# An RWKV-6 attention with a two-layer network behind it: the same 1124 steps in another order, 39 of them on another engine

## The chip, the cores and the metric

The kernel runs on one core of a Trainium2 chip. The metric is the device time of one execution in microseconds (us). One execution was also profiled, and its trace gives the begin and length of each instruction on each engine. PE is TensorE (matrix products and transposes), DVE is VectorE, ACT is ScalarE, POOL is GpSimd, and SP is the engine that issues the transfers (DMA).

## What is computed

The first part is a recurrence with one state of 48 x 48 for each of 4 batches and 8 heads, over 768 positions. The second part takes the result as 3072 rows of 384 numbers through two matrices with a leaky ReLU between them.

```python
for t in range(S):                       # S = 768; B = 4, H = 8, D = 48
    cur = einsum('bhd,bhe->bhde', u * k_t, v_t)
    y[:, :, t] = einsum('bhd,bhde->bhe', r_t, state + cur)
    state = w_t[..., None] * state + einsum('bhd,bhe->bhde', k_t, v_t)
x = y.transpose(0, 2, 1, 3).reshape(3072, 384)
h = x @ w_in                             # 384 x 2048
out = maximum(0.01 * h, h) @ w_out       # 2048 x 384
```

## The kernel before

**Chunks.** The positions are cut into pieces of 128 rows, so that a piece of all eight heads is one tile of 128 x 384. Inside a piece the recurrence becomes matrix products. The logarithms of the decays w are taken (L508, L718) and summed down the rows by a product with a triangular matrix (L518, L724). ACT takes exponentials of the sums (L551 in `pair`, L750 and L754 in `single`). DVE multiplies r and k with them (the four multiplications at L407 of a `pair`, two of a `single` chunk). PE transposes the products (L418), they are copied out of PSUM to `g` or `rkT` by ACT (L425) or DVE (L423), and PE forms the scores (L632, L864). DVE masks the scores (L644, L795), PE multiplies them with v (L657, L836), and the bonus of u comes from POOL (L437, L441, L449) and a DVE sum (L445). The state `s` is carried from one chunk to the next: `sb` is the state times its decay (L602, L782), PE sums the new one into PSUM (L591, L609, L805), and a copy, a "keep", puts it back into SBUF (L617 on DVE or L619 on ACT in `pair`; L818 and L820 in `single`).

**Pairs and singles.** The function `pair` does the first chunks of two batches at once, with 64 rows each, at the head of the program. `single` does one chunk of 128 rows for later ones. Its transposed r and k come either through PE and a copy, or by a DMA transpose (L771) that SP issues. The result y (L482, L688) has to be transposed too, by PE (L468, copied by L473 on DVE or L475 on ACT) or by a DMA transpose (L849).

**The network.** For each block of rows, "up" is the product with w_in (L1030), ACT applies the leaky ReLU (L1045), and "down" is the product with w_out (L1060), whose result is copied to `o` and stored (L1077). The last seven blocks use another form for the second layer, `seven`, which makes seven products out of sums of matrix pieces: DVE makes the sums of pieces of 128 x 1024 (L941), PE multiplies (L960), the results are added by DVE (L981) after copies (L974, L976), and L1013 stores them. The weights are loaded as float32 (L318, L323) and cast to bfloat16 by POOL (L340), DVE (L342) or ACT (L344).

**What sets the order.** Each piece of work is a step in a list of 1124, with the engines that may do it. A table `ORDER` gives the order in which the steps are issued, and a table `FORCE` the engine of those that have a choice. A planner walks `ORDER`. It gives each step a buffer of its pool (11 buffers `in`, 8 of PSUM `ps`, 5 `rk`, 4 `g`, 5 `o` and others), by the times that it works out. The instructions of an engine are then executed in the order in which they were issued, so one that has to wait holds everything behind it on its engine. All transfers are issued by SP, in one such row too, but for the small load of u (L363). Until 24 us of the planned time, products of a tile of zeros (L1099) are put into planned gaps of PE; nothing reads what they make.

Of the kernel before, what the change touches and what calls it, by code (L numbers as in the profile page):

```python
# [22 lines left out]
class Plan:  # L23
# [76 lines left out]
ORDER = [1122, 0, 1, 2, 3, 4, 5, 6, 7, 11, 14, 20, 12, 18, 15, 17, 16, 13, 19, 21, 8, 22, 25, 26, 27, 23, 36,  # L100
    40, 24, 9, 28, 31, 29, 30, 41, 42, 37, 38, 32, 33, 48, 50, 49, 51, 53, 52, 63, 67, 70, 76, 68, 74, 75, 71,
    73, 72, 69, 77, 10, 35, 39, 34, 44, 45, 54, 46, 47, 43, 56, 57, 55, 60, 64, 78, 79, 80, 81, 92, 96, 65, 87,
    84, 85, 86, 93, 94, 97, 98, 88, 89, 61, 62, 82, 83, 58, 59, 107, 108, 109, 104, 105, 106, 127, 128, 129,
    727, 728, 729, 730, 125, 126, 725, 726, 66, 91, 90, 95, 99, 100, 101, 110, 111, 112, 113, 116, 130, 131,
    731, 732, 132, 733, 734, 119, 120, 719, 720, 114, 115, 121, 122, 721, 722, 145, 149, 133, 135, 134, 753,
    754, 747, 748, 117, 118, 751, 752, 151, 152, 154, 153, 102, 103, 735, 765, 766, 761, 762, 767, 768, 741,
    146, 156, 161, 123, 124, 763, 764, 755, 147, 155, 162, 163, 174, 178, 723, 724, 749, 750, 159, 160, 1123,
    157, 158, 769, 180, 181, 182, 183, 165, 166, 167, 136, 138, 137, 736, 770, 756, 139, 141, 140, 737, 176,
    184, 186, 187, 148, 150, 164, 170, 171, 168, 169, 175, 185, 190, 191, 192, 203, 207, 771, 209, 212, 211,
    210, 213, 214, 222, 757, 742, 172, 173, 142, 144, 143, 188, 189, 204, 216, 218, 743, 223, 227, 205, 215,  # L110
    219, 220, 777, 778, 781, 782, 775, 776, 744, 745, 758, 759, 229, 230, 234, 231, 233, 232, 194, 195, 196,
    738, 739, 779, 780, 783, 224, 236, 241, 225, 235, 242, 243, 177, 179, 193, 199, 200, 263, 267, 217, 239,
    240, 772, 773, 197, 198, 245, 760, 206, 208, 221, 237, 238, 784, 201, 202, 269, 270, 274, 272, 271, 273,
    285, 226, 228, 244, 246, 248, 247, 256, 255, 264, 276, 281, 785, 789, 790, 295, 299, 786, 787, 791, 792,
    251, 252, 350, 793, 794, 259, 260, 301, 304, 303, 302, 306, 305, 317, 797, 257, 258, 253, 254, 265, 275,
    282, 283, 249, 250, 296, 308, 313, 297, 307, 314, 315, 261, 262, 266, 284, 268, 327, 746, 409, 798, 795,
    796, 352, 298, 316, 300, 817, 818, 805, 806, 803, 804, 354, 331, 875, 876, 877, 878, 279, 280, 277, 278,
    811, 812, 819, 309, 310, 815, 816, 311, 312, 799, 333, 336, 335, 334, 349, 351, 365, 366, 800, 801, 286,
    288, 287, 807, 808, 318, 320, 319, 809, 825, 291, 292, 356, 357, 813, 323, 324, 293, 367, 810, 820, 325,
    326, 329, 814, 337, 339, 826, 821, 328, 345, 346, 347, 359, 361, 363, 360, 362, 294, 831, 832, 788, 407,  # L120
    411, 408, 425, 426, 427, 387, 391, 389, 467, 358, 369, 330, 348, 332, 469, 835, 836, 837, 838, 388, 402,
    403, 353, 368, 355, 364, 413, 414, 417, 416, 418, 525, 539, 289, 290, 419, 420, 827, 338, 340, 843, 822,
    844, 823, 448, 833, 834, 341, 342, 393, 394, 396, 828, 829, 343, 344, 398, 400, 373, 374, 415, 447, 395,
    406, 397, 399, 847, 841, 842, 404, 462, 848, 370, 371, 372, 379, 380, 421, 422, 845, 846, 839, 840, 853,
    321, 322, 429, 375, 376, 423, 424, 854, 383, 384, 855, 449, 463, 464, 401, 377, 378, 740, 385, 386, 390,
    392, 405, 410, 412, 428, 430, 432, 439, 431, 440, 849, 861, 862, 468, 482, 483, 526, 540, 802, 450, 465,
    452, 524, 470, 472, 504, 859, 451, 860, 471, 869, 870, 381, 382, 453, 454, 458, 460, 455, 456, 466, 457,
    459, 461, 850, 851, 852, 856, 867, 868, 473, 474, 477, 478, 476, 475, 486, 441, 442, 871, 872, 435, 436,
    443, 444, 865, 866, 437, 438, 863, 864, 445, 873, 874, 433, 505, 480, 479, 481, 446, 899, 528, 508, 900,
    901, 902, 909, 910, 903, 904, 510, 512, 513, 913, 914, 530, 532, 533, 543, 506, 905, 906, 911, 912, 541,  # L130
    519, 520, 507, 509, 434, 523, 857, 487, 879, 880, 884, 883, 881, 882, 484, 485, 580, 594, 579, 824, 560,
    830, 858, 774, 531, 534, 511, 514, 496, 515, 497, 500, 516, 895, 907, 489, 517, 518, 547, 885, 887, 535,
    488, 492, 536, 908, 919, 548, 537, 538, 501, 502, 493, 494, 886, 915, 916, 917, 890, 888, 892, 889, 891,
    503, 495, 949, 559, 893, 894, 950, 918, 921, 922, 521, 574, 522, 935, 583, 896, 947, 527, 529, 542, 544,
    545, 546, 553, 581, 595, 561, 575, 582, 584, 936, 563, 948, 636, 616, 552, 923, 924, 898, 943, 944, 941,
# [998 lines left out]
```

## Time and profile before

| | us |
|---|---|
| median of 3 runs | 178.72 |
| lowest and highest | 178.51 and 179.15 |
| profiled execution | 178.69 |
| its span in the trace | 177.0 |
| PE busy within the span | 170.4 |

The 1.7 us between the span and the time of the profiled execution lie before the first and behind the last recorded instruction. In the rows of the timeline, a row has a start, the time that the group lasts, the engine, the source line, the operation, its output and inputs, the count, and in brackets how long the engine was idle before it and what ended that. Views that group by window give the busy time of each engine and, in brackets, its number of instructions.

### The profile page before, as it was taken

Reading aid. Unit: us, or ns where it says so; the run is one execution under the profiler, and the core shown is the slowest. Engines: PE = TensorE matmul, PEld = TensorE weight load, DVE = VectorE, ACT = ScalarE, POOL = GpSimd, SP = SyncE. Lnnn points to the kernel's source line nnn. Section 1 sums busy time; section 2 is a strip of 40 time slices with the busy share of each in tenths; the row PEclk is TensorE's granted clock in tenths of the full one; section 3 lists DMA queues with packets and bytes.
Section 4 is the critical chain, followed back from the end, with each engine's and each line's share of the span. In section 5 each row is a group of like instructions: output and inputs, shape, how many; then the busy total and the mean of one; then the engine's idle time right before and its main releaser. Section 6 shows DMA issues by size and latency. Waiting matters only on the chain.

```text
span 177.0 us, 5530 instructions
## 1 busy us (share of the span) xinstructions
PE 170.4 (96%) x2155; PEld 139.9 (79%) x2158; DVE 143.5 (81%) x299; ACT 114.0 (64%) x263; POOL 107.3 (61%) x143
## 2 busy tenths in 40 slices
PE   7999999999999999999999999999999998999993
PEld 2566779867768877777779899899899997799992
DVE  7498935267599899889879999999999999956662
ACT  5676769734677794796379964676769950178500
POOL 5989946486749859879599093391693959100000
PEclk9999999999999999999999999999999999999999
DMA  5999999999999999999999999996999897432104
GB/s 138 261 271 340 350 300 195 351 231 199 201 206 195 191 199 227 163 201 179 198 206 195 197 208 209 163 222 124 210 194 196 188 226 78 118 101 80 44 26 157
DMA packets 115885, 34.25 MB, mean 194 GB/s; under 512 B 108305, under 2 KB 115090, under 8 KB 115858
## 3 DMA queue, kind: packets, MB, share of 16 engines
q1 hardware_dynamic: 115856, 33.89, 93.1%
q8 instruction: 17, 0.28, 0.7%
q14 instruction: 10, 0.08, 0.2%
q10 hardware_dynamic: 2, 0.00, 0.0%
HBM read 25.17 MB, written 4.72 MB: 169 GB/s over the span
## 4 chain that ended last, share of the span: by engine, by line
PE 69%; DVE 15%; ACT 5%; issue 4%; DMA 3%; POOL 2%; DVEq 0%; SPq 0%; ACTq 0%
PE ps L1030 30%; PE ps L1060 13%; PE ps L960 10%; DVE rk L407 3%; DMA rkT<-rk 3%; PE ps L864 3%; DVE in L941 2%; PE ps L418 2%; ACT g L425 2%; PE ps L724 1%; PE ps L836 1%; DVE ci L736 1%; PE ps L518 1%; DVE dg L445 1%; ACT ps L750 1%
## 5 line engine op out<-in xcount | busy, mean ns | idle before, releaser
L1030 PE MATMUL ps<-xT,w_in_b 128*128 128x256 bf16 (+1 forms) x672 | 70.8, 258 | 0.3 <-DVE rk L407 0.2
L1045 ACT ACTIVATE g<-ps 128x512 bf16<-128x512 f32 x96 | 54.4, 598 | 18.1 <-PE ps L1030 16.0
L1030 PEld LDWEIGHTS <-w_in_b 128*128 128x128 bf16 x672 | 56.9, 98 | 7.8 <-issue 0.6
L437 POOL TENSOR_TENSOR ru<-in,ub 128x384 f32<-128x384 f32 x24 | 24.3, 1017 | 13.1 <-DMA in<-in_k_dram 7.0
L1060 PE MATMUL ps<-w_out_b,g 128*128 128x384 bf16 x160 | 31.4, 326 | 0.0
L407 DVE TENSOR_TENSOR rk<-in,ps 128x384 bf16<-128x384 f32 x48 | 24.8, 547 | 6.1 <-ACT ps L754 2.3
L782 POOL TENSOR_TENSOR sb<-s,a 128x384 bf16<-128x384 f32 x18 | 15.6, 875 | 16.6 <-ACT a L745 8.1
L795 DVE TENSOR_TENSOR m<-ps,maskb 128x512 bf16<-128x512 f32 x40 | 25.1, 682 | 0.3 <-PE ps L864 0.2
L441 POOL TENSOR_TENSOR ru<-ru,in 128x384 f32<-128x384 f32 x24 | 23.8, 1000 | 2.1 <-DMA in<-in_r_dram 1.1
L1060 PEld LDWEIGHTS <-g 128*128 128x128 bf16 x160 | 14.1, 97 | 6.8
L449 POOL TENSOR_TENSOR vs<-in,dg 128x384 f32<-128x384 f32 x20 | 17.4, 874 | 3.0 <-DMA in<-in_v_dram 2.1
L960 PEld LDWEIGHTS <-g 128*128 128x128 bf16 x224 | 18.3, 98 | 0.2
L976 ACT COPY o<-ps 128x192 f32<-128x192 f32 x18 | 5.8, 320 | 17.5 <-PE ps L960 15.5
L960 PEld LDWEIGHTS <-in 128*128 128x128 bf16 x168 | 13.6, 98 | 1.9 <-DVE in L941 1.4
L445 DVE TENSOR_REDUCE dg<-ru 128x8 f32<-128x384 f32 x24 | 12.9, 545 | 1.9 <-POOL ru L441 1.7
L457 POOL CAST vb<-in 128x384 bf16<-128x384 f32 x24 | 12.7, 534 | 2.2 <-DMA in<-in_v_dram 2.2
L981 DVE TENSOR_TENSOR o<-ps,o 128x192 f32<-128x192 f32 x35 | 11.6, 351 | 1.9 <-ACT o L976 1.1
L482 DVE TENSOR_TENSOR y<-ps,vs 128x384 bf16<-128x384 f32 x20 | 10.9, 553 | 2.4 <-PE ps L836 2.3
L754 ACT ACTIVATE ps<-ci 128x384 f32<-128x384 f32 x20 | 9.8, 493 | 4.7 <-DVE ci L736 4.1
L718 ACT ACTIVATE lw<-in 128x384 bf16<-128x384 f32 x20 | 9.9, 521 | 4.1 <-DMA in<-in_w_dram 4.1
L736 DVE TENSOR_TENSOR ci<-ps,lw 128x384 f32<-128x384 f32 x20 | 10.9, 551 | 1.8 <-PE ps L724 1.1
L960 PE MATMUL ps<-in,in 128*128 128x192 bf16 x112 | 11.4, 247 | 0.5 <-DVE in L941 0.5
(105 smaller groups left out, 258.8 us busy)
## 6 DMA issues: line engine op xcount, KB each, us to landing
out_dram<-o SPq DMA_DIRECT2D x23, 192.0 KB, 2.8
in<-in_w_dram SPq DMA_DIRECT2D x20, 192.0 KB, 4.7
in<-in_k_dram SPq DMA_DIRECT2D x20, 192.0 KB, 4.2
in<-in_r_dram SPq DMA_DIRECT2D x20, 192.0 KB, 4.2
in<-in_v_dram SPq DMA_DIRECT2D x20, 192.0 KB, 4.1
in<-in_moe_w_out_dram SPq DMA_DIRECT2D x4, 768.0 KB, 6.9
in<-in_moe_w_in_dram SPq DMA_DIRECT2D x2, 768.0 KB, 9.7
in<-in_moe_w_in_dram SPq DMA_DIRECT2D x4, 384.0 KB, 8.1
```

Of the source, the lines that this page charges most:

```text
L407: (nc.gpsimd if e == "POOL" else nc.vector).tensor_tensor(out=o, in0=x, in1=i, op=ALU.mult)
L437: lambda e: nc.gpsimd.tensor_tensor(out=ru.t[:], in0=kv(), in1=ubv, op=ALU.mult),
L441: lambda e: nc.gpsimd.tensor_tensor(out=ru.t[:], in0=ru.t[:], in1=rv(), op=ALU.mult),
L445: lambda e: nc.vector.tensor_reduce(out=dg.t[:], in_=ru.t[:], axis=AX.X, op=ALU.add),
L449: lambda e: nc.gpsimd.tensor_tensor(out=vs.t[:], in0=vv(), in1=dg.t[:].unsqueeze(2).to_broadcast([128, H, D]), op=ALU.mult),
L457: {"POOL": 0.56}, lambda e: nc.gpsimd.tensor_copy(out=vb.t[:], in_=vv()),
L782: lambda e: nc.gpsimd.tensor_tensor(out=sb.t[:].rearrange("p g a d -> p (g a) d"), in0=s_in.t[:].rearrange("p g a d -> p (g a) d"), in1=a_ ...
L795: lambda e, par=par: nc.vector.tensor_tensor(out=m.t[:, par, :, :], in0=sc[par].t[:].rearrange("p (g t) -> p g t", g=NP), in1=maskb[:].uns ...
L960: nc.tensor.matmul(o(), lhsT=x()[:, i, :], rhs=y()[:, i, :], start=fresh, stop=(stop and i == ii[-1]), skip_group_check=True)
L1030: nc.tensor.matmul(hp.t[:, a * N : (a + 1) * N], lhsT=w_in_b[:, t, (j + a) * 128 : (j + a + 1) * 128], rhs=xb.t[:, t, 0:N], start=(a == 0 ...
L1045: lambda e, hp=hp, g=g, j=j, J=J, N=N: nc.scalar.activation(out=g.t[:, j : j + J, 0:N], in_=hp.t[:, 0 : J * N].rearrange("p (a n) -> p a n ...
L1060: nc.tensor.matmul(op.t[:, 0:DM], lhsT=g.t[:, j, off : off + 128], rhs=w_out_b[:, j, :], start=(j == 0), stop=(j == NJ - 1))
```

## The change

The functions, the 1124 steps and the pools are the same. The tables `ORDER` and `FORCE` hold other numbers.

```diff
@@ -97,71 +97,71 @@
-ORDER = [1122, 0, 1, 2, 3, 4, 5, 6, 7, 11, 14, 20, 12, 18, 15, 17, 16, 13, 19, 21, 8, 22, 25, 26, 27, 23, 36,
...
+ORDER = [0, 1122, 1, 2, 4, 3, 5, 6, 7, 11, 13, 12, 18, 19, 14, 15, 16, 17, 20, 21, 8, 22, 25, 40, 36, 23, 24,
...
-FORCE = {4: "ACT", 6: "DVE", 24: "ACT", 27: "ACT", 30: "DVE", 33: "ACT", 47: "ACT", 57: "ACT", 59: "DVE", 60:
+FORCE = {4: "DVE", 6: "DVE", 24: "ACT", 27: "ACT", 30: "ACT", 33: "ACT", 47: "DVE", 57: "ACT", 59: "ACT", 60:
...
-    "DVE", 118: "DVE", 120: "POOL", 122: "POOL", 124: "POOL", 126: "POOL", 128: "ACT", 129: "POOL", 131: "ACT",
+    "ACT", 118: "DVE", 120: "POOL", 122: "POOL", 124: "DVE", 126: "DVE", 128: "ACT", 129: "ACT", 131: "POOL",
...
```

Steps 24 to 33 are the copies of the first transposed tiles, 47 is the first keep, 57 to 62 are copies of the second transposed tiles and of the first transposed y, and 113 to 144 are casts of the weights. The change has 12 products of zeros more at the head (47 for 35). 39 steps are done by another engine than before, all of them copies and casts; POOL has six casts of weights fewer in sum. Everything else is as often there as before.

**The head, DVE.** Behind the masks of the first pair's scores (`m0`, `m1`). `sb0` is the decayed state, `s0` the kept one, `rk2` and `rk3` the second pair's r and k times their exponentials. Before:

```order
L644 TENSOR_TENSOR m1_117<-ps5_156,mask2_65 128x512
L602 TENSOR_TENSOR sb0_128<-ps2_153,a0_119 128x384
L407 TENSOR_TENSOR rk2_94<-in2_76,ps4_155 128x8x48
L407 TENSOR_TENSOR rk3_95<-in2_76,ps7_158 128x8x48
L407 TENSOR_TENSOR rk2_94<-in3_77,ps3_154 128x8x48
L407 TENSOR_TENSOR rk3_95<-in3_77,ps1_152 128x8x48
L423 COPY g1_137<-ps7_158 128x512
```

Now:

```order
L644 TENSOR_TENSOR m1_117<-ps2_153,mask2_65 128x512
L602 TENSOR_TENSOR sb0_128<-ps6_157,a0_119 128x384
L617 COPY s0_122<-ps3_154 128x384
L407 TENSOR_TENSOR rk2_94<-in3_77,ps1_152 128x8x48
L407 TENSOR_TENSOR rk3_95<-in3_77,ps7_158 128x8x48
L407 TENSOR_TENSOR rk3_95<-in2_76,ps4_155 128x8x48
L407 TENSOR_TENSOR rk2_94<-in2_76,ps5_156 128x8x48
```

The keep of the first state now stands on DVE ahead of the four multiplications of the second pair, and the copy L423 behind them is no longer next to them.

**The head, ACT.** From the first keep to the first leaky ReLU (L1045). Before:

```order
L619 COPY s0_122<-ps6_157 128x384
L688 CAST y2_134<-ps5_156 128x384
L688 CAST y3_135<-ps2_153 128x384
L425 COPY g1_137<-ps4_155 128x4x128
L425 COPY g1_137<-ps3_154 128x512
L425 COPY g1_137<-ps6_157 128x4x128
L344 CAST w_in_b_72<-in4_78 128x3x256
L1045 ACTIVATE g2_138<-ps6_157 128x512
```

Now:

```order
L688 CAST y2_134<-ps2_153 128x384
L688 CAST y3_135<-ps6_157 128x384
L425 COPY g1_137<-ps3_154 128x512
L425 COPY g1_137<-ps1_152 128x4x128
L475 COPY xT0_140<-ps2_153 128x3x128
L425 COPY g1_137<-ps4_155 128x512
L344 CAST w_in_b_72<-in4_78 128x3x256 x2
L1045 ACTIVATE g2_138<-ps7_158 128x512
```

The keep L619 is gone from ACT. Of the three transposed tiles L425 the third now stands behind a copy of a transposed y (L475), and two casts of w_in stand ahead of the first leaky ReLU, where one stood.

**The transfers, SP.** The loads around the first DMA transpose (L771, the r and k of the first chunk that has them transposed by a DMA). Before:

```order
L708 DMA in2_76<-in_r_dram 128x8x48
L708 DMA in6_80<-in_k_dram 128x8x48
L708 DMA in6_80<-in_r_dram 128x8x48
L708 DMA in1_75<-in_v_dram 128x8x48
L708 DMA in7_81<-in_w_dram 128x8x48
L771 DMA_TRANSPOSE rkT2_99<-rk1_93 128x8x128
L1077 DMA out_0_dram<-o3_149 128x384
```

Now:

```order
L708 DMA in4_78<-in_r_dram 128x8x48
L708 DMA in3_77<-in_r_dram 128x8x48
L708 DMA in3_77<-in_k_dram 128x8x48
L708 DMA in4_78<-in_v_dram 128x8x48
L708 DMA in8_82<-in_w_dram 128x8x48
L708 DMA in9_83<-in_w_dram 128x8x48
L771 DMA_TRANSPOSE rkT2_99<-rk1_93 128x8x128
L708 DMA in3_77<-in_v_dram 128x8x48
```

Between the last loads of r or k and the transpose stand now a load of v and two of w, where one of v and one of w stood, and the store L1077 behind it has gone further back. Counted from the head of the list, the transpose stands two places later (number 36 for 34).

**The last chunks, DVE.** Sums for the products of `seven` (L941), the masks of the last two chunks (L795), the sums of their y (L482), and the sums of results (L981). Before:

```order
L482 TENSOR_TENSOR y1_133<-ps7_158,vs0_112 128x384
L445 TENSOR_REDUCE dg2_111<-ru1_108 128x8
L941 TENSOR_TENSOR in0_74<-in0_74,g1_137 128x1024
L981 TENSOR_TENSOR o0_146<-ps1_152,o1_147 128x192
L941 TENSOR_TENSOR in0_74<-g1_137,in0_74 128x1024
L795 TENSOR_TENSOR m1_117<-ps3_154,maskb_64 128x512
L981 TENSOR_TENSOR o1_147<-ps6_157,o4_150 128x192
```

Now:

```order
L941 TENSOR_TENSOR in2_76<-in2_76,g1_137 128x1024
L482 TENSOR_TENSOR y1_133<-ps1_152,vs3_115 128x384
L482 TENSOR_TENSOR y0_132<-ps5_156,vs2_114 128x384
L795 TENSOR_TENSOR m0_116<-ps2_153,maskb_64 128x512
L795 TENSOR_TENSOR m0_116<-ps4_155,maskb_64 128x512
L795 TENSOR_TENSOR m1_117<-ps5_156,maskb_64 128x512
L795 TENSOR_TENSOR m1_117<-ps1_152,maskb_64 128x512
L941 TENSOR_TENSOR in2_76<-g1_137,in2_76 128x1024
L981 TENSOR_TENSOR o4_150<-ps0_151,o2_148 128x192
```

Before, only an L981 stood between the last two L941 of this sub-block; now two L482 and four masks do.

18 lines of the change are left out of this document (9 added, 9 removed), and 106 rows, old and new, of the table ORDER.

## The prediction, made before the changed kernel ran

> **What bounds the kernel now.** I read the view by window first, to see which engine is full in which stretch, then the timeline of the head, then PE's gaps along the chain of waits.
>
> ```profile
> core 0: us, PE busy (x) PEld busy (x) DVE busy (x) ACT busy (x) POOL busy (x), PEclk, DMA share, GB/s
> 0.00:19.30 19.30, 17.11 (x221) 9.96 (x224) 15.08 (x43) 13.24 (x28) 16.07 (x32) 1.00 1.05 263
> 53.00:100.00 47.00, 47.00 (x572) 37.53 (x571) 42.12 (x80) 35.07 (x84) 36.91 (x46) 1.00 1.09 195
> 127.00:152.40 25.40, 24.44 (x321) 22.11 (x321) 25.19 (x48) 14.36 (x39) 19.00 (x23) 1.00 0.97 176
> ```
>
> From 53 to 100 us PE, at full clock (1.00), has no gap in 47.00 us, so nothing that DVE, ACT or POOL do there can shorten the run, and what comes later there costs nothing until it is late by more than its slack. From 127 to 152.4 us DVE is full as well (25.19 of 25.40). Up to 19.3 us PE is busy too, but with products of zeros among the rest; the network, most of its work, hasn't begun, and the head is a chain over PE, DVE and ACT. So an order can gain or lose in three kinds of place only: in the head, at PE's gaps, and behind the last product. The DMA share is about 1.0 in all three rows, so a transfer that stands later in the queue also lands later.
>
> **The head, +1.4.** The timeline shows the chain up to the first product of the network.
>
> ```profile
> 6.66 0.47 ACT L551 ACTIVATE ps<-ps 128x384 f32<-128x384 f32 x1 [1.12 <-PE ps L518]
> 7.81 1.95 DVE L407 TENSOR_TENSOR rk<-in,ps 128x384 bf16<-128x384 f32 x4 [1.87 <-ACT ps L551]
> 8.13 0.84 ACT L551 ACTIVATE ps<-ps 128x384 f32<-128x384 f32 x2
> 9.32 1.71 ACT L425 COPY g<-ps 128x512 bf16<-128x512 bf16 x3 [0.34 <-PE ps L418]
> 11.08 0.64 PE L632 MATMUL ps<-g 48*64 48x128 bf16 x32 [0.17 <-ACT g L425]
> 14.13 0.56 DVE L602 TENSOR_TENSOR sb<-ps,a 128x384 bf16<-128x384 f32 x1
> 14.60 1.94 DVE L407 TENSOR_TENSOR rk<-in,ps 128x384 bf16<-128x384 f32 x4
> 15.29 0.34 PE L609 MATMUL ps<-sb,ident 128*128 128x384 bf16 x1
> 15.66 0.48 ACT L619 COPY s<-ps 128x384 f32<-128x384 f32 x1 [1.32 <-PE ps L609]
> 18.37 0.90 ACT L344 CAST w_in_b<-in 128x768 bf16<-128x768 f32 x1
> 18.59 0.64 PE L632 MATMUL ps<-g 48*64 48x128 bf16 x32
> 19.32 1.92 PE L1030 MATMUL ps<-xT,w_in_b 128*128 128x256 bf16 x16
> ```
>
> - Before, one exponential could start at 6.66, on the first running sum that was ready. In the changed order the sum that two of them need is made third, so the four L551 (0.42 each, one behind another) and the two small ones (L541) come later and end near 9.35, where the last ended at 8.13 + 0.84 = 8.97. The third multiplication waits for its exponential, and the four end near 10.4 instead of 7.81 + 1.95 = 9.76: +0.6.
> - All four transposed tiles are copied by ACT, where DVE took one. The copies take 0.57 each (1.71 for three), and the last puts the scores near 11.8 (11.08): +0.7, mostly the same 0.6.
> - The keep on DVE has no cover. It needs PE's L609, which ran at 15.29 while DVE was already at the second pair's multiplications; these now stand behind it. L609 can come right behind `sb` (14.13 + 0.56 + 0.7 late = 15.4) and takes 0.34, and a copy like L619 takes 0.48: the multiplications start near 16.2 and end near 18.1, where they ended at 16.54. That makes +1.6. Queued behind the waiting keep are also the sums L445 and the next masks; PE's transposes L418 wait for the multiplications.
> - One of the second pair's copies goes back to DVE, but ACT has the copy of a transposed y among its three: scores near 19.95 (18.59), +1.4.
> - Two casts of 0.90 stand on ACT ahead of the first leaky ReLU. The first ends shortly before L1030 can start, near 20.7; the second lies beside L1030's first products.
>
> So 20.7 - 19.32 = 1.4. Bounds: 0.7 if the keep's wait is hidden by slack between the two pairs, and 2.0 if the second cast delays products too (0.6 of its 0.9). I take 1.4, since each link has a row. The twelve further products of zeros cost nothing: they stand where PE waits for this chain, and without that cover they would cost under 0.4 each.
>
> **35 to 53 us, -0.9 and +0.7.** PE has three gaps here. Its rows overlap, so I take each by its starts: a group could have begun when the one before it had run its usual time, which the chain shows where PE is full.
>
> ```profile
> 42.64 1.50 PE L1030 MATMUL ps<-xT,w_in_b 128*128 128x128 bf16 x24
> 44.31 0.83 PE L1030 MATMUL ps<-xT,w_in_b 128*128 128x128 bf16 x12 [0.16 <-DVE rk L407]
> 48.35 0.81 PE L1060 MATMUL ps<-w_out_b,g 128*128 128x384 bf16 x4
> 49.20 0.49 PE L836 MATMUL ps<-vb,m 128*128 128x48 bf16 x8
> 49.81 0.40 PE L418 MATMUL ps<-ident,rk 128*128 128x128 bf16 x4
> 54.94 0.67 PE ps L1030 x12
> 58.61 0.65 PE ps L1060 x4
> 56.82 0.20 PE ps L836 x8
> ```
>
> 42.64 + 2 x 0.67 = 43.98 against 44.31; 48.35 + 0.65 = 49.00 against 49.20; 49.20 + 0.20 = 49.40 against 49.81. That is 0.33 + 0.20 + 0.41 = 0.94. They are waits for chains of chunks whose loads came late. With PE 1.4 late at this place, these chains have the time to be done: -0.94, bounds -0.94 and 0.
>
> The DMA transpose is new in the way.
>
> ```profile
> L771 SPq DMA_TRANSPOSE rkT<-rk x1: 2007/2007/2007, 46.1 to 46.1; - x1
> DMA to landing us min/median/max: 5.6/5.6/5.6
> 52.31 0.55 PE ps L864 x16
> ```
>
> Issued at 46.1, it landed near 51.7, and the scores that need it ran at 52.31: 0.6 us of slack. Two more loads of 128 x 384 float32 now stand ahead of it. At 195 GB/s (the row from 53 to 100) one takes 196,608 B / 195 GB/s = 1.0 us, so it lands near 53.7. PE, 1.4 late and without 0.94 of gaps, gets there near 52.8: a wait of 0.9. If the queue is a load ahead by then, the wait is 0. I take 0.7, nearer the first, since the share of DMA leaves no room. The whole of PE's row waits behind those scores. Bounds 0 and 0.95.
>
> **127 to 152.4 us, -1.3 and +0.5.** DVE is full, and PE waits for sums of it twice.
>
> ```profile
> 149.01 0.83 PE L960 MATMUL ps<-w_out_b,in 128*128 128x192 bf16 x8
> 150.38 0.84 PE L960 MATMUL ps<-in,in 128*128 128x192 bf16 x8 [0.53 <-DVE in L941]
> 151.61 0.83 PE L960 MATMUL ps<-w_out_b,in 128*128 128x192 bf16 x8 [0.40 <-DVE in L941]
> 118.40 0.66 PE ps L960 x8
> L941 DVE TENSOR_TENSOR in<-g 128x1024 bf16<-128x1024 bf16 (+1 forms) x8 | 4.9, 618 | 3.9 <-ACT g L1045 3.9
> L482 DVE TENSOR_TENSOR y<-ps,vs 128x384 bf16<-128x384 f32 x20 | 10.9, 553 | 2.4 <-PE ps L836 2.3
> L795 DVE TENSOR_TENSOR m<-ps,maskb 128x512 bf16<-128x512 f32 x40 | 25.1, 682 | 0.3 <-PE ps L864 0.2
> ```
>
> 149.01 + 0.66 = 149.67 against 150.38, and 151.04 against 151.61: gaps of 0.71 and 0.57. From the scores of the last two chunks to the first of these sums DVE had 97 instructions, and has 90 now: four L941 (0.62), two L482 (0.55) and three others of a tile of 128 x 384 fewer, two small copies more. That is about 4 us less of DVE's work beside the same work of PE, so both waits go: -1.28. In their place four masks and two L482 stand between the last two L941: from one sum to the next 4 x 0.63 (25.1 / 40) + 2 x 0.55 + 0.62 = 4.2, while PE has five products of 0.66 = 3.3 between them. The 0.9 is a wait if the first sum is just in time, and none if it is 0.9 early. I take 0.5, the middle: less work ahead makes the sum early, but the masks wait for scores of PE. Bounds 0 and 0.9; what is queued behind is the last sums, and behind them PE's products.
>
> **Three small ones.**
>
> ```profile
>   PEld L864: 0.2, 1
> DMA to landing us min/median/max: 2.3/2.6/3.5
> out_dram<-o SPq DMA_DIRECT2D x3, 192.0 KB, 1.9
> out_dram<-o SPq DMA_DIRECT2D x1, 96.0 KB, 1.6
> ```
>
> The first row says who waited for the transposes L771: PE's scores, once (at 113.35), for 0.2. The transpose in question has moved forward: -0.2, bounds -0.2 and 0. The second row is that of the transposes L849. The sum L482 of a late chunk stands three DVE instructions later (some 1.8 us at 0.6), and its L849 lands later by as much. PE has products of other blocks to do meanwhile, which hide most of it: +0.2, bounds 0 and 0.7 (one group of eight products is 0.66). Behind the last product, the last store is a whole tile (1.9 to landing) instead of a half (1.6): +0.3, with no cover.
>
> **Sum.** 1.4 - 0.94 + 0.7 - 1.28 + 0.5 - 0.2 + 0.2 + 0.3 = +0.7 on the profiled execution of 178.69 (span 177.0 and 1.7 around it, which stays): 179.4. The median, 178.72, is 0.03 from that execution.
>
> **The rivals.**
> - *Faster, 177.5.* In the head the keep's wait is hidden, so +0.7, and there is no wait for the transpose or the last sums: 178.69 + 0.7 - 0.94 - 1.28 - 0.2 + 0.2 + 0.3. It decides if the first L1030 starts before 20.0. For it: all of PE's gaps have a cause that a later PE or a shorter row on DVE removes. Against it: L602, L609, keep and L407 are a chain with no cover.
> - *No change, 178.6.* The late head is given back: 1.4 - 0.94 - 1.28 + 0.3 - 0.2, and half of the new waits, 0.6. For it: a late PE shifts against transfers and DVE alike. Against it: the gaps it lives on end there; from 53 to 100 us PE has none.
> - *Much slower, 181.3.* The new waits all reach their upper bounds, since DVE and the queue are full where they arise: 2.0 - 0.94 + 0.95 - 1.28 + 0.9 + 0.7 + 0.3 = 2.6. Against it: each has some slack ahead of it.
> - *Fetches of instructions, 179.9.*
>
> ```profile
> q8 instruction: 17, 0.28, 0.7%
> ```
>
> Queue 8 took 17 packets in 0.007 x 16 x 177 = 19.8 us, 1.2 each. PE has no gap beyond those named, so none of the fetches stops it and there is nothing to gain; one that a new order moves to where nothing is queued ahead of it on PE would cost up to 1.2: 178.69 + 1.2. [...]
>
> **Chances.** Forecast 0.38, faster 0.27, no change 0.18, much slower 0.12, fetches 0.05. A difference of 0.3% (0.54 us) is about what a measurement of this kernel can tell from none: "same" is 178.2 to 179.3. It takes 0.04 from the forecast's lower edge and gives 0.02 to faster: same 0.20, faster 0.29, slower 0.51. The range for 8 in 10 goes from 177.1 (the faster rival with L849 at nothing, and 0.2 for the scatter of the runs) to 181.3. The forecast's own is 178.9 to 180.2.
>
> **What would show it.** The first L1030 near 20.7; DVE idle for some 0.3 us before the keep L617, with PE's L609 as releaser; no gap of PE at 44 to 50 us, but one before the L864 near 53 with the transpose as releaser; before the last products only one wait for L941. The forecast is wrong if the first L1030 comes before 20.0, if PE has gaps between 53 and 100 us, where I have none, or if its time without the products of zeros differs by over 0.5 us.

## The result: 1.1% slower, and where the time went

The changed kernel took 180.79 us in the median of six runs (179.97 to 181.58), the old one 178.92 beside it (178.51 to 179.31). The ratio is 1.0106 with a 95% interval of 1.0069 to 1.0144, so it is slower by 1.9 us, give or take 0.7. The profiled execution took 181.17 with a span of 179.5. The forecast was 179.4 in a range of 177.1 to 181.3. The sign is right and the time lies in the range, but above the forecast's own 178.9 to 180.2, and nearer to the rival "much slower" (181.3) than to the forecast. Of its terms some were right and some were not.

First the view by window, as before the change (busy us of each engine and its number of instructions, granted clock, DMA share, GB/s):

```profile
0.00:19.30 19.30, 16.84 (x200) 9.82 (x204) 14.54 (x42) 12.51 (x27) 15.35 (x31) 1.00 1.06 266
53.00:100.00 47.00, 45.99 (x550) 35.45 (x548) 40.44 (x77) 32.86 (x80) 35.68 (x46) 1.00 1.14 198
127.00:152.40 25.40, 25.40 (x342) 23.44 (x339) 25.03 (x50) 15.94 (x41) 16.01 (x18) 1.00 1.06 194
```

From 53 to 100 us PE now has a gap of 1.0 us where it had none, and from 127 to 152.4 it is full where it had lost 1.0 (24.44 of 25.40).

To see where PE's time goes I use one number. **PE's loss** at a group of products is the start of the group, less the usual time of all of PE's work that stands ahead of it (each kind of product at the pace that it has where PE is full; products of zeros are not work). The work is the same in both orders, so the losses can be compared between kernels, although the groups stand in another order. The level of a loss depends on the pace that is taken for the short products of the head, so only differences are given; with the median time from one start to the next as pace they come out the same within 0.02.

| at | before: start | changed: start | loss, changed less before | of it since the row above |
|---|---|---|---|---|
| first L1030 | 19.32 | 20.45 | 1.13 | +1.13 |
| scores (L864) behind the first DMA transpose | 52.24 | 54.21 | 1.90 | +0.77 |
| scores (L864) of the chunk near 127 us | 126.34 | 129.29 | 3.60 | +1.70 |
| scores (L864) of the last chunk | 152.38 | 152.41 | 2.01 | -1.59 |
| from there to the end of the span | | | 2.50 | +0.49 |

The sum is +2.50, the difference of the two spans (179.5 and 177.0). The medians differ by less, 1.9; the runs of the changed kernel are spread over 1.6 us, those of the old one beside it over 0.8 (178.13 to 181.20 in a later batch of 23).

**The head** in the timeline of the changed kernel:

```profile
7.59 0.55 DVE L407 TENSOR_TENSOR rk<-in,ps 128x384 bf16<-128x384 f32 x1 [1.18 <-ACT ps L551]
8.72 1.48 DVE L407 TENSOR_TENSOR rk<-in,ps 128x384 bf16<-128x384 f32 x3 [0.58 <-ACT ps L551]
9.10 2.50 ACT L425 COPY g<-ps 128x512 bf16<-128x512 bf16 x4
11.65 0.64 PE L632 MATMUL ps<-g 48*64 48x128 bf16 x32 [0.23 <-ACT g L425]
15.52 0.56 DVE L617 COPY s<-ps 128x384 f32<-128x384 f32 x1 [0.41 <-PE ps L609]
15.99 1.94 DVE L407 TENSOR_TENSOR rk<-in,ps 128x384 bf16<-128x384 f32 x4
19.57 1.56 ACT L344 CAST w_in_b<-in 128x768 bf16<-128x768 f32 x2
19.76 0.64 PE L632 MATMUL ps<-g 48*64 48x128 bf16 x32
20.45 2.22 PE L1030 MATMUL ps<-xT,w_in_b 128*128 128x256 bf16 x18
```

Each link is there: DVE waits 0.58 for an exponential in the middle of the four multiplications, ACT copies all four tiles, the keep waits 0.41 for PE's L609, and the second four multiplications end at 17.93. The scores stand at 11.65 and 19.76, against 11.8 and 19.95 in the prediction.

**PE's gaps up to 53 us** have not gone, but stand at other places:

```profile
34.13 1.15 PE L1060 MATMUL ps<-w_out_b,g 128*128 128x384 bf16 x6 [0.24 <-DVE w_out_b L342]
38.01 0.36 PE L836 MATMUL ps<-vb,m 128*128 128x48 bf16 x8 [0.20 <-POOL vb L457]
38.54 0.40 PE L864 MATMUL ps<-rkT 48*128 48x128 bf16 x8 [0.17 <-ACT rkT L425]
44.39 0.37 PE L836 MATMUL ps<-vb,m 128*128 128x48 bf16 x8 [0.32 <-ACT g L1045]
```

By the losses they are 0.41, 0.36, 0.33 and 0.49, together 1.6; the old kernel had 0.94. The releasers of the first two are a cast of w_out and a cast of v; each had waited for its load, or stood behind a cast that had. The scores behind the DMA transpose at 54.21 show no wait.

**At 84 us** PE waits for a DMA transpose, the largest of its new gaps (1.13 by the loss). The two rows of the changed kernel, and behind them the same transpose and its scores before:

```profile
79.31 1.27 SPq L771 DMA_TRANSPOSE rkT<-rk  x1
84.42 0.40 PE L864 MATMUL ps<-rkT 48*128 48x128 bf16 x8 [0.96 <-DMA rkT<-rk]
75.42 2.20 SPq L771 DMA_TRANSPOSE rkT<-rk  x1
81.66 0.62 PE L864 MATMUL ps<-rkT 48*128 48x128 bf16 x16
```

Another 0.42 of the 1.70 arose at 108 us, at a product of L960 that waited for ACT's copy L976.

**The late chunks** show neither of the two waits for L941:

```profile
150.28 0.68 DVE L941 TENSOR_TENSOR in<-in,g 128x1024 bf16<-128x1024 bf16 x1
154.21 0.68 DVE L941 TENSOR_TENSOR in<-g,in 128x1024 bf16<-128x1024 bf16 x1
150.98 1.49 PE L960 MATMUL ps<-in,in 128*128 128x192 bf16 x16
155.10 0.82 PE L960 MATMUL ps<-w_out_b,in 128*128 128x192 bf16 x8
```

The two L941 are 3.9 apart, as forecast (4.2). The products that need them are 4.1 apart, not 3.3: scores and products with the state stand between them too, so that DVE was in time (the first sum ended at 150.96, for a product at 150.98). What made the waits before is seen in the old kernel, in the rows of the two sums and of POOL beside them:

```profile
148.94 2.07 POOL L449 TENSOR_TENSOR vs<-in,dg 128x384 f32<-128x384 f32 x2
149.02 1.30 DVE L941 TENSOR_TENSOR in<-in,g 128x1024 bf16<-128x1024 bf16 x1
150.51 1.04 DVE L941 TENSOR_TENSOR in<-g,in 128x1024 bf16<-128x1024 bf16 x1
```

The sums took 1.30 and 1.04 us there, and 0.68 each in the changed kernel, where POOL did nothing at these times. That is 0.98 of the 1.28 of the two waits.

**The end.** The last sum ends at 176.05 + 0.36 = 176.41, 3.1 ahead of the end of the span, against 2.6 before (174.40 and 177.0).

### The profile page after: what moved, and what is told of

Read it like the earlier page. It is cut to its first block, busy times and chain, and to the rows that moved or that the text cites. A ratio compares the mean times of both kernels' runs of the same rounds, so it can differ in the third digit from the quotient of the medians.

```text
span 179.5 us, 5547 instructions
## 1 busy us (share of the span) xinstructions
PE 171.1 (95%) x2167; PEld 141.0 (79%) x2170; DVE 144.2 (80%) x301; ACT 118.2 (66%) x267; POOL 102.8 (57%) x137
## 4 chain that ended last, share of the span: by engine, by line
PE 63%; DMA 11%; DVE 8%; issue 6%; POOL 5%; ACT 5%; SPq 1%; ACTq 0%; POOLq 0%; DVEq 0%
PE ps L1030 25%; PE ps L960 18%; PE ps L1060 6%; DMA in<-in_moe_w_out_dram 4%; DMA in<-in_r_dram 4%; DMA rkT<-rk 3%; PE ps L864 2%; PE ps L836 2%; DVE in L910 2%; PE ps L831 2%; DVE rk L407 1%; POOL ru L441 1%; POOL sb L782 1%; PE ps L805 1%; PE ps L468 1%
## 5 line engine op out<-in xcount | busy, mean ns | idle before, releaser
L1030 PE MATMUL ps<-xT,w_in_b 128*128 128x256 bf16 (+1 forms) x672 | 70.3, 257 | 0.1
L1045 ACT ACTIVATE g<-ps 128x512 bf16<-128x512 f32 x96 | 55.3, 600 | 12.5 <-PE ps L1030 10.8
L1030 PEld LDWEIGHTS <-w_in_b 128*128 128x128 bf16 x672 | 56.6, 98 | 7.6 <-ACT w_in_b L344 0.4
L437 POOL TENSOR_TENSOR ru<-in,ub 128x384 f32<-128x384 f32 x24 | 24.8, 1037 | 20.0 <-DMA in<-in_k_dram 17.1
L1060 PE MATMUL ps<-w_out_b,g 128*128 128x384 bf16 x160 | 30.8, 326 | 0.2 <-DVE w_out_b L342 0.2
L441 POOL TENSOR_TENSOR ru<-ru,in 128x384 f32<-128x384 f32 x24 | 24.6, 1028 | 5.0 <-DMA in<-in_r_dram 4.0
L795 DVE TENSOR_TENSOR m<-ps,maskb 128x512 bf16<-128x512 f32 x40 | 25.0, 680 | 0.7 <-PE ps L864 0.6
L449 POOL TENSOR_TENSOR vs<-in,dg 128x384 f32<-128x384 f32 x20 | 16.6, 829 | 10.6 <-DMA in<-in_v_dram 7.6
L960 PEld LDWEIGHTS <-g 128*128 128x128 bf16 x224 | 18.6, 98 | 0.3
L782 POOL TENSOR_TENSOR sb<-s,a 128x384 bf16<-128x384 f32 x18 | 15.9, 892 | 4.8 <-ACT a L745 2.8
L457 POOL CAST vb<-in 128x384 bf16<-128x384 f32 x24 | 12.0, 504 | 7.0 <-DMA in<-in_v_dram 6.3
L981 DVE TENSOR_TENSOR o<-ps,o 128x192 f32<-128x192 f32 x35 | 11.6, 351 | 4.8 <-DMA out_dram<-o 3.9
L976 ACT COPY o<-ps 128x192 f32<-128x192 f32 x15 | 4.7, 320 | 16.0 <-PE ps L960 11.6
L960 PEld LDWEIGHTS <-in 128*128 128x128 bf16 x168 | 13.9, 98 | 0.6 <-issue 0.3
L750 ACT ACTIVATE ps<-ps 128x384 f32<-128x384 f32 x20 | 9.5, 482 | 6.2 <-DVE ci L736 5.9
L482 DVE TENSOR_TENSOR y<-ps,vs 128x384 bf16<-128x384 f32 x20 | 10.7, 551 | 3.3 <-PE ps L836 1.8
L1099 PE MATMUL ps<-zeros 128*128 128x128 bf16 (+1 forms) x44 | 10.1, 340 | 1.5 <-DVE zeros L261 1.3
L960 PE MATMUL ps<-in,in 128*128 128x192 bf16 x112 | 11.2, 246 | 0.3 <-ACT o L976 0.3
```

Source lines behind the costliest of these rows:

```text
L437: lambda e: nc.gpsimd.tensor_tensor(out=ru.t[:], in0=kv(), in1=ubv, op=ALU.mult),
L441: lambda e: nc.gpsimd.tensor_tensor(out=ru.t[:], in0=ru.t[:], in1=rv(), op=ALU.mult),
L449: lambda e: nc.gpsimd.tensor_tensor(out=vs.t[:], in0=vv(), in1=dg.t[:].unsqueeze(2).to_broadcast([128, H, D]), op=ALU.mult),
L457: {"POOL": 0.56}, lambda e: nc.gpsimd.tensor_copy(out=vb.t[:], in_=vv()),
L782: lambda e: nc.gpsimd.tensor_tensor(out=sb.t[:].rearrange("p g a d -> p (g a) d"), in0=s_in.t[:].rearrange("p g a d -> p (g a) d"), in1=a_ ...
L795: lambda e, par=par: nc.vector.tensor_tensor(out=m.t[:, par, :, :], in0=sc[par].t[:].rearrange("p (g t) -> p g t", g=NP), in1=maskb[:].uns ...
```

## The experiments

In the diffs OLD and NEW are the two orders, with the engines that belong to them. Each ratio is against runs of the old kernel taken beside it; their medians lay between 178.92 and 179.08.

### Head and rest exchanged

```diff
-ORDER = NEW
+ORDER = OLD[:131] + [i for i in NEW if i not in OLD[:131]]
```

> The changed kernel with the head of the old order: the first 131 steps of the old table, with their engines, then all other steps as the changed table has them. Theory (the chain at the head costs 1.1 of PE, and the loads of weights and r, k, v that the head's casts on ACT hold up cost 0.7 more by 45 us): the first L1030 comes back to 19.3, both are gone, and the time is the changed one less 1.8, about 179.0. Rival (only the chain counts; the gaps between 34 and 45 us come from the order after the head): 179.7. Rival (a later PE had saved waits further on, which now come back): no gain, 180.8.

Measured: 182.14, ratio 1.0144 (1.0092 to 1.0195). The head came back and nothing was gained (the changed kernel's ratio is 1.0106). PE's rows, of the first product of the network, the largest new gap and the scores behind the first DMA transpose:

```profile
19.33 0.94 PE L1030 MATMUL ps<-xT,w_in_b 128*128 128x256 bf16 x7
28.85 0.48 PE L724 MATMUL ps<-lw,trev 128*128 128x384 bf16 x2 [0.84 <-ACT lw L718]
54.16 0.62 PE L864 MATMUL ps<-rkT 48*128 48x128 bf16 x16
```

PE was 1.12 us earlier at L1030 and 0.05 earlier at L864 (54.21 in the changed kernel). What the head won was waited off between them. The rival without a gain held. At the end PE lost another 1.3 before one product at 155.58, waiting for the cast of a v, which the changed kernel did not.

```diff
-ORDER = OLD
+ORDER = NEW[:122] + [i for i in OLD if i not in NEW[:122]]
```

> The old kernel with the head of the changed order: the first 122 steps of the changed table, with their engines, then all other steps as the old table has them. Theory (the head is lost for good): first L1030 near 20.45, time 178.9 + 1.1 = 180.0, and more if the loads are late too. Rival (the gaps of the old order at 44, 49, 150 and 151 us, 2.2 together, take the delay in): 178.9.

Measured: 180.50, ratio 1.0064 (1.0031 to 1.0098), the 1.1 us of the theory. But not by its way: L1030 started at 20.18, and then PE waited at 25.88 for the cast of w_in that this mixture puts on ACT, and at 28.64 for a copy (losses of 1.04 and 0.61). The gaps of the old rest at 44 and 49 us were gone, as the rival said, and both waits for L941 were there again (0.76 and 0.57).

```diff
-FORCE[47] = "ACT"   # old kernel, one keep
+FORCE[47] = "DVE"
```

> The old kernel with one change of engine: the first state's keep on DVE instead of ACT, ahead of the four multiplications of the second pair, which have to wait for PE's L609. The prediction priced that link at about 1 us: first L1030 near 20.2 instead of 19.32, on both theories. Theory (the transfers set the pace up to 53 us): the scores at 52.24 stay within 0.2 and the time within 0.3 of before. Rival (what the head loses is lost for good, as the prediction had it): the time rises by 0.9.

Measured: 179.42, ratio 1.0028 (0.9997 to 1.0058). PE's rows of the same two places:

```profile
20.20 1.03 PE L1030 MATMUL ps<-xT,w_in_b 128*128 128x256 bf16 x8
52.63 0.62 PE L864 MATMUL ps<-rkT 48*128 48x128 bf16 x16
```

The price of the link was right: L1030 is 0.88 late, at the 20.2 that was expected. At the scores only 0.39 of it is left, and of the time 0.5, with an interval that holds 0. So more than half of this delay was taken in by 53 us; the bound of 0.2 in the expectation was too narrow. It did not stay so: by 84 us PE's loss was 1.27 above that of the old kernel; 0.65 of it was lost at 57.7 and 58.2 us.

The opposite is seen in a run made for another reason. Its first 115 us are those of the old kernel in order and engines:

```diff
-ORDER = OLD
+ORDER = OLD[:854] + [i for i in NEW if i not in OLD[:854]]
```

> The old order up to 127 us (its first 854 steps, with their engines), then the rest in the changed order. Theory (the changed order of the last third saves the two waits for L941, 0.71 and 0.57, wherever it begins, and costs 0.45 behind the last product): 178.9 - 1.5 + 0.45 = 177.9, which is below both kernels. Rival (the waits went because PE was late in the changed kernel, not by the order): 178.9 to 179.4.

```profile
18.50 1.27 PE L1030 MATMUL ps<-xT,w_in_b 128*128 128x256 bf16 x10
41.15 0.32 PE L724 MATMUL ps<-lw,trev 128*128 128x384 bf16 x1 [1.60 <-ACT lw L718]
52.33 0.62 PE L864 MATMUL ps<-rkT 48*128 48x128 bf16 x16
```

In this execution the head happened to be 0.82 earlier than in the profile of the old kernel (19.32). At 41.15 PE waited 1.6 for the logarithms of a w that had just landed, and at L864 it was 0.09 later (52.24). In the old order an earlier head is worth nothing at 53 us. In the changed order it is worth nearly all: of two kernels below that have its order up to 70 us, one began its first L1030 at 19.95 and had these scores at 53.74, the other at 20.57 and 54.50 (20.45 and 54.21 in the changed kernel). What this run says of its own question follows below.

### What the transfers do up to 53 us

```diff
 SP's row of the old kernel (numbers of steps)
-142 204 223 205 224 225 177 263 217 760 206 226 264 295
+177 204 223 142 205 225 224 206 295 263 217 760 226 264
```

Step 142 is the last load of w_out, 204, 205 and 224, 225 are k and r of two chunks, 177 and 206 are v, 223, 263 and 295 are w, 217 is the DMA transpose and 760 a store.

> The old kernel with only SP's row moved: the same loads and the DMA transpose in the changed kernel's order, with two loads more ahead of the transpose. Theory (transfers set the pace): the transpose lands near 53.7 instead of 51.7, the scores run near 54 instead of 52.24, and the time rises by 1.3 to 1.8, to about 180.5. Rival (slack takes the two loads in): the time stays within 0.5 of before.

Measured: 181.37, ratio 1.0116 (1.0083 to 1.0150). So 2.1 us are lost by moving transfers alone, with no other engine's row touched. PE's largest gap and the scores:

```profile
47.16 1.79 PE L1060 MATMUL ps<-w_out_b,g 128*128 128x384 bf16 x8 [2.27 <-POOL w_out_b L340]
55.26 0.62 PE L864 MATMUL ps<-rkT 48*128 48x128 bf16 x16
```

The scores are 3.0 later than before; of that 2.4 arose at 47.16, where PE waits for the cast of the last w_out. That load was issued at 40.35 instead of 35.63, behind three others. The rest goes with a granted clock of PE of 0.50 from 48.2 to 51.6 us; the other five executions, with a mean clock of 0.999 or 1.000, lost their 2.1 without that. The direction was expected; the place was not, since the theory looked at the transpose.

```diff
 SP's row of the changed kernel
-177 204 223 142 205 225 224 206 295 263 217
+204 223 142 205 224 225 177 263 217 206 295
```

> The changed kernel with only SP's row moved: the eleven loads and the DMA transpose from the v of the second single chunk on stand in the order of the old kernel, so that the transpose has the v of one chunk and the w of another no longer ahead of it, and k comes ahead of that v. No step changes its engine. Theory (up to 53 us the transfers set PE's pace, whatever the head does: the old head in front of the changed rest brought the scores behind the first DMA transpose to 54.16 against 54.21): these scores come near 53 and the time falls by 1.0, to 179.8. Rival (the gaps from 34 to 45 us come from casts and buffers, not from the loads' order): the scores stay near 54.2 and the time at 180.8.

Measured: 189.58, ratio 1.0544 (1.0497 to 1.0591). Neither theory nor rival had this. The load of step 177, the cast and the product that need it, then a multiplication of DVE and the transpose:

```profile
45.49 0.80 SPq L708 DMA_DIRECT2D in<-in_v_dram  x1
50.02 0.51 POOL L457 CAST vb<-in 128x384 bf16<-128x384 f32 x1 [7.50 <-DMA in<-in_v_dram]
50.58 0.48 PE L836 MATMUL ps<-vb,m 128*128 128x48 bf16 x8 [6.43 <-POOL vb L457]
54.56 0.54 DVE L407 TENSOR_TENSOR rk<-in,ps 128x384 bf16<-128x384 f32 x1
55.13 1.56 SPq L771 DMA_TRANSPOSE rkT<-rk  x1
```

The v of step 177 was moved from the first to the seventh of these places: issued at 45.49 instead of 36.35. In the changed rows its product stands at 44.4, so PE waited 6.4 for it, and DVE and POOL waited too (6.4 and 7.5). The transpose has no part in this gap; it stands behind this load. But SP came to it at 47.4 and stood there for 7.8 us, until 55.13, just behind the multiplication of the DVE that had been waiting; all loads behind it waited too, and the DMA ran empty from about 50 us (its share from 53 to 60 us is 0.51, where the changed kernel has 1.24). The gap is 6.6 by the loss; PE lost another 2.7 up to 84 us (0.9 in the changed kernel), much of it with a granted clock of 0.50 from 47.4 to 54.2. As a test of the theory the run decides nothing: the old order of SP's row doesn't fit the changed rows of the other engines.

```diff
 SP's row of the changed kernel: the first load of w_out
-174 145 147 146 175 133
+174 133 145 147 146 175
```

> The changed kernel with the first load of w_out two places after the last of w_in, as the old order has it, and so between the loads of w for two chunks, instead of behind five loads of w, k and r in a row. Theory (five loads in small pieces in a row leave SP waiting for room in the queue, so that nothing is under way near 24.5 us, where the DMA share falls to a tenth; this hole of about 1 us is one of the things that the changed order loses up to 53 us): the hole goes, the first down at 34.1 doesn't wait for its cast, the scores at 54.2 come to 53.3, time 180.0. Rival (the loads of w, k and r come later by the 2 us of the weight, and PE's gaps only move): 180.8 or more.

Measured: 182.71, ratio 1.0198 (1.0166 to 1.0230). The hole that this was to fill is plain in the changed kernel; the view of the DMA from 24 to 26 us (busy tenths in 40 slices of 0.05 us):

```profile
DMA  9999997555441011111111578889999999999998
```

The old kernel has 8 or 9 in each of these slices. That SP waits for room in the queue, as the theory has it, is not shown: the waits that the trace of the changed kernel has for SP from 17 to 26 us, of 2.7, 0.8 and 0.6, are for casts on ACT and POOL. The wait for the first down, at 34.13, went as the theory said. But the w of a chunk came later, and PE waited at 29.28 for its logarithms (0.94) instead; the scores stood at 54.15, where they had stood at 54.21. The rival held. Another 0.9 was lost at 156 us before a product that waited for the cast of a v; it was no part of either.

```diff
 SP's row of the changed kernel
-177 204 223 142 205
+204 205 177 223 142
```

> The changed kernel with the load of r for the third single chunk ahead of the last load of w_out of 768 KB and of a v, where it stood behind both. Theory (this r, landed at 47.1 against 45.5 in the old kernel, sets when the chain of that chunk goes on, and with it the transpose at which SP waits 2.7 us): it lands near 44, SP's wait shrinks, the scores at 54.2 come to 53.5, time 180.1. Rival (the weight's cast comes later by 1 us and PE waits for that): 181.

Measured: 181.41, ratio 1.0123 (1.0086 to 1.0159). The r landed at 43.2 instead of 47.1. PE's gaps before L836 at 44.77 and L805 at 46.61 grew to 0.97 and 0.95, both after a leaky ReLU on ACT, and the scores came at 55.58. The rival's figure held, not its mechanism: the weight's cast was later (it ended at 49.28), but no gap is put down to it. What came later as well were two loads: the v landed at 44.05 instead of 42.15, and its cast ended just before the first of these products; the w landed at 45.52 instead of 43.84, and ACT waited 0.83 for it ahead of the second leaky ReLU.

```diff
-FORCE = NEW
+FORCE = NEW, but for the casts of weights (steps 119 to 144) as in OLD
```

> The changed kernel with the casts of weights on the engines that the old table gives them (POOL for six that are on ACT or DVE now, ACT for one that is on POOL); the order of the steps stays. Theory (SP's loads wait for buffers that the casts on ACT release late, and the gaps of DMA at 24 and 35 us make PE wait at 34, 38 and 44 us): the wait of 2.7 us of a load for L344 on SP goes, the gaps of PE from 34 to 45 us shrink from 1.6 to under 1.0, time about 180.1. Rival (the casts cost only as a chain on ACT ahead of the first leaky ReLU): 0.2 less, 180.6. Rival (POOL becomes late with the casts, which were moved off it for that reason): 181 or more.

Measured: 181.52, ratio 1.0124 (1.0074 to 1.0174). The gaps from 34 to 45 us fell to almost nothing, as the theory had it, but PE waited in one piece before:

```profile
26.02 1.16 PE L1030 MATMUL ps<-xT,w_in_b 128*128 128x256 bf16 x9 [1.73 <-ACT w_in_b L344]
```

That is the one cast which the old table has on ACT, step 131. The scores behind the transpose came at 54.33. By the wait before that L1030, it is no clean test of the other casts.

### The transpose at 84 us

```diff
 SP's row of the changed kernel
-774 467 448 390 449 408 409 746 364
+364 774 467 448 390 449 408 409 746
```

Steps 774 and 746 are stores, the other six that 364 passes are loads.

> The changed kernel with one step moved: the DMA transpose that PE waited for at 84.4 us (1.1 lost) is issued as soon as its r and k are ready, ahead of six loads and a store that stood between. Theory: the gap at 84 us goes and nothing else, time 0.6 to 1.1 less, 179.7 to 180.2. Rival (the loads that come later by the transpose make POOL and DVE late, and PE waits there instead): no gain.

Measured: 186.00, ratio 1.0366 (1.0330 to 1.0402). The largest of SP's waits for this transpose, and PE's gap:

```profile
SPq L771 <- DVE rk L407: 9.4, 6, 5.2
86.77 0.60 PE L418 MATMUL ps<-ident,rk 128*128 128x128 bf16 x4 [4.37 <-DVE rk L407]
```

SP was 5.2 us ahead of DVE here, since loads are issued early: it came to the transpose at 70.1 and waited that long for DVE. The loads behind were issued up to 5 us later (409 at 82.1 instead of 77.3), and PE waited 4.4 for a multiplication that needs one of them (the k of step 408, landed at 85.4 instead of 80.9). The gap is 4.5 by the loss. From 86.8 to 90.2 us the granted clock was 0.50, and PE lost another 1.5 up to 92 us.

```diff
-448 390 449 408 409 746 364
+448 390 449 364 408 409 746
```

> The changed kernel with the DMA transpose that PE waited for at 84.4 us three places earlier in SP's row, ahead of two loads of r and k and a store, and not ahead of all six loads as in the run in which SP then waited 5.2 us at it for DVE's multiplications (70.1 to 75.4) and held the loads behind it. Theory (a transpose in SP's row costs on both sides: too late and PE waits for it, too early and SP waits at it with all loads behind): here its r and k are ready when SP comes to it at about 76.4, it lands near 81, PE's gap of 1.1 at 84 goes and no other comes; 179.7 to 180.3. Rival (each load behind it is as urgent): the loads of r and k, each about 1 us later, make a gap of the same size; no gain.

Measured: 180.94, ratio 1.0107 (1.0065 to 1.0149), no gain. The transpose was issued at 76.8, landed at 80.7, and PE did not wait for it. It waited here:

```profile
84.82 0.40 PE L418 MATMUL ps<-ident,rk 128*128 128x128 bf16 x4 [1.61 <-DVE rk L407]
```

That is the r of step 409, now behind the transpose: the loss is 1.77 where it was 1.13. The rival held. In these two orders there is a gap of over 1 us at this place whichever of the two comes first. I take it that one transfer too many is wanted at this time; no run here takes one away.

### The late chunks, and a try to beat both

The run with the old order up to 127 us took 179.66, ratio 1.0051 (1.0011 to 1.0091). Neither wait for L941 is in it. PE's lateness is not what removes them: the old kernel with the new loads was late by 3 us at these sums and had both waits (0.54 and 0.40 in its rows). What they follow is POOL. In the 14 traces L941 on a whole tile took 0.67 to 0.69 us in each of 257 cases without work on POOL beside it; all 45 that took over 0.70, up to 1.55, had POOL's L449, L457 or L782 beside them. And in the old order with the keep on DVE, POOL was idle during these two sums:

```profile
150.17 0.67 DVE L941 TENSOR_TENSOR in<-in,g 128x1024 bf16<-128x1024 bf16 x1
151.03 0.67 DVE L941 TENSOR_TENSOR in<-g,in 128x1024 bf16<-128x1024 bf16 x1
150.90 0.83 PE L960 MATMUL ps<-in,in 128*128 128x192 bf16 x8
151.76 0.83 PE L960 MATMUL ps<-w_out_b,in 128*128 128x192 bf16 x8
```

PE lost 0.09 and 0.20 there in place of 0.71 and 0.57, with the old rows of DVE. So the larger part of the two waits is what POOL's work beside them adds to the two sums, and the changed order has it elsewhere.

In the run with the old order up to 127 us the join cost more than that: PE's loss rose by 1.7 between 127 and 134 us (by 0.1 in the old kernel), the largest piece a product that waited for DVE's multiplications at 132.22, and from the last sum (174.83) to the end of the span (177.6) it took 2.8, 0.2 more than in the old kernel.

```diff
-ORDER = OLD
+ORDER = OLD[:775] + [i for i in NEW if i not in OLD[:775] and i not in OLD[1073:]] + OLD[1073:]
```

> The old order for its first 775 steps (to about 115 us), the changed order from there to about 165 us, and the old order again for the last 51 steps, so that the last store is again a half tile. Theory (the changed order of the late chunks removes the waits of 0.71 and 0.57 for L941 by itself, as the run with the change from 127 us showed, in which PE lost 1.2 where the two orders were joined instead; the whole tile at the end costs 0.45): no gap at the last products, 2.6 us from the last product to the end of the span, and if the join here costs 0.5 or less, 178.0 to 178.5, below before. Rival (DVE sets the pace from 127 to 155 us in any order, so that what is not lost at the L941 is lost at the join or later): 178.8 to 179.5, no better than before.

Measured: 179.55, ratio 1.0016 (0.9986 to 1.0046), no difference from the old kernel. PE's row at the join, and the last sum:

```profile
116.09 0.33 PE L805 MATMUL ps<-vb,rk 128*128 128x96 bf16 x4 [1.19 <-POOL vb L457]
174.60 0.36 DVE L981 TENSOR_TENSOR o<-ps,o 128x192 f32<-128x192 f32 x1 [0.29 <-PE ps L960]
```

The waits for L941 are gone, the span ends at 177.5, 2.6 behind the last sum as in the old kernel, and 1.35 are lost at 116 us for the cast of a v. Twice about as much as the 1.28, or more, was lost at the join instead. Whether an order without that wait can be found, or DVE's full row brings it back anywhere, as the rival says, these two runs don't tell.

## Why the prediction was right in sign and too small

**The head: right as a chain, open as a price.** It was given +1.4 with 20.7 for the first L1030; measured are +1.13 and 20.45. The two scores were met within 0.2. But the sum added it to the end, less 0.94 of gaps. The old head before the new rest gained nothing, and an old head that ran 0.82 early gained nothing by 53 us. Of a delay of 0.88 by the keep alone, 0.39 was left at 53 us, 1.27 at 84 us, and 0.5 in the time, with an interval from nothing to 1.0. In the changed order, 0.5 of an earlier head came through to 53 us nearly whole. What the head is worth is set by what PE meets behind it; one price for it, as in the sum, is not shown.

**35 to 53 us: the step that failed.** "With PE 1.4 late at this place, these chains have the time to be done: -0.94." This took the landing of the loads as fixed while PE moved. In the changed order the loads moved too: the five small loads in a row leave the DMA a tenth busy for half a microsecond at 24.8, the w_out and v that PE needs at 34 and 38 us land just before it needs them, and gaps of 1.6 stand where those of 0.94 had been. The term, with the transpose's, was -0.24 in the sum and +0.77 in the trace. That the row of transfers alone can do this is shown in the old kernel, where moving it cost 2.1 us. Which of the moves made the 0.77 is not shown: two changes of that row and one of the casts left the scores between 54.15 and 55.58.

**The transpose near 53 us: right landing, no wait.** Forecast to land at 53.7, it landed at 53.77. PE was expected at 52.8 and came at 54.21, held by the gaps before it. The +0.7 had the right price of 1.0 us for a load, and the wrong guess of who would be later.

**53 to 127 us: the second failure.** The prediction argued that PE has no gap from 53 to 100 us and priced nothing there but a gain of 0.2. It said that a gap in this stretch would prove it wrong, and +1.70 arose from 53 to 127, 1.13 of it at 84 and 0.42 at 108 us. The reasoning took the old slack for the new: in the old kernel the transpose of this chunk was issued at 75.42 and landed 1.85 ahead of its use. In the new SP's row it is issued at 79.31, behind six loads and two stores that were issued from 70.9 us on, and landed at 84.37. An order that changes every row has to be searched for its tight transfers along the whole row, not only at the old gaps.

**127 to 152 us: right that both waits go, too cautious about a new one.** -1.28 + 0.5 + 0.2 for the transposes L849 was forecast, and -1.59 measured. But the reason given, a shorter row on DVE, is not what the traces show. From the scores near 127 us to the first of these sums DVE had 43 instructions before and 41 now, and it stays as busy (25.03 of 25.40 us, before 25.19). The two sums themselves were long, 1.30 and 1.04 us beside POOL's L449, and that accounts for 0.98 of the 1.28; so the size of this term was met partly by luck. The new wait did not come because PE's work between the two products was 4.1, not the 3.3 of five products of L960: products of the two chunks stand among them.

**The end: right.** +0.3 was forecast for a whole tile in the last store, and 0.49 measured; with the old tail it was gone.

**Fetches of instructions** decided nothing: 17 packets in both profiles, and no gap of PE over 0.3 us that hasn't an engine or a transfer as its releaser. Neither shows PE waiting for a fetch, so the 1.2 us of that rival stays an estimate.

The twelve further products of zeros were put at nothing; no run leaves them out, so that stays untested.

So the forecast of +0.7 against +2.5 in the traces (1.9 in the medians) is a sum in which two terms about transfers were too low by 1.0 and 1.9, and those of the head, the late chunks and the end too high by 1.1 together. The right sign is largely luck. The head, the late chunks and the end, where the prediction saw what happens, sum to +0.03; all of the slowdown arose in the two stretches that it had as small gains (-0.24 and -0.2). Two of the signs that it named failed in the same places: there was to be no gap between 44 and 50 us, and one of 0.49 stands at 44.39; there was to be none between 53 and 100 us.

## What to carry to other kernels

A gap is not a fixed price that a later engine pays off: ask what the awaited thing waits for in turn, and when that is a transfer, go through the issuing queue's new row and give each transfer a landing time of its own before pricing a move of anything else. A transfer that needs a computed tile has two prices in a queue of loads, one if it stands late (1.1 us at 84 us here) and one, for all that stands behind it, if it stands early (4.5 us). When an engine is awaited, first see whether its instruction took its usual time, and what ran beside it, before blaming the length of its row (the sums of 1.30 and 1.04 us beside POOL, 0.68 without). In this schedule, in which loads, PE and DVE are each full in some stretch, a part taken over from another order brought its waits with it (1.7 us lost at one join, 1.35 at the other); compare the losses at fixed pieces of work, not the gaps.

## What was not expected of the hardware

One transfer in SP's row that had to wait stopped all loads behind it: with 5.2 us at a transpose, loads were issued up to 5 us later and PE lost 4.5.

A long gap of PE cost twice here: behind the one of 4.4 us PE lost another 1.5. Gaps of 6.4, 4.4 and 2.3 us are each followed, or overlapped, by a stretch in which the granted clock was 0.50 (47.4 to 54.2, 86.8 to 90.2 and 48.2 to 51.6 us); beside gaps of 1.73, 1.60 and 1.61 us (at 26.02, 41.15 and 84.82, in three kernels) it stayed at 1.00. After the gap of 2.3 only the profiled execution shows it.

DVE's work was longer beside some of POOL's: L941 took 0.68 us alone and up to 1.55 beside L449, L457 or L782. Beside POOL's L437 or L441 alone it stayed at 0.67 to 0.69 in 25 cases.

And the head varies from execution to execution by itself: with the same instructions in the same order, the first L1030 started at 19.32, 18.50 and 18.61 in three kernels, with the scores behind the first DMA transpose at 52.24, 52.33 and 52.37. In six kernels with the changed head it started between 19.89 and 20.57. Prices of the head that rest on one execution each, the 0.88 of the keep among them, have that scatter.
